# Feature maps scaled crosswise, sets normalised in pairs, and a Gram certificate placed later, in a kernel that mixes linear and softmax attention

## The chip, the cores and the metric

The kernel runs on one core of a Trainium2 chip. The metric is the device time of one execution in microseconds (us). The engines are PE (matrix multiplication; PEld is its weight loading), DVE (the vector engine), ACT (activations), POOL (GpSimd) and SP, which issues transfers.

## What is computed

Two attention layers read the same x (2048 tokens, 512 features, 32 heads of 16) and a gate mixes them for each token.

```python
def reference(A_x, A_wqkv, A_w_phi, A_wo, B_x, B_wqkv, B_wo, gate_w):
    x = A_x
    g = _sigmoid((x * gate_w).sum(-1, keepdims=True))
    # A, linear attention; q, k, v = heads of x @ A_wqkv
    pq, pk = q @ w_phi, k @ w_phi                      # per head
    phi_q = concat([softmax(pq), softmax(-pq)], -1)    # 16 + 16 features
    phi_k = concat([softmax(pk), softmax(-pk)], -1)
    kv, z = phi_k^T v, phi_k.sum(keys)
    a = (phi_q kv) / (phi_q z + 1e-6) @ A_wo
    # B, softmax attention; q, k, v = heads of x @ B_wqkv
    b = softmax(q k^T / 4) v @ B_wo
    return g * a + (1 - g) * b
```

## The kernel before

**Softmax attention in sets.** The work is cut into 32 sets. A set is one chunk of 512 queries, one group of eight heads and, of these, the four of one parity. A set has 16 blocks, one for each 128 keys. For a block PE computes the scores of four heads (L1241) into PSUM; then the exponential is taken in one of two ways. On ACT it is two activations of 128x1024 (L1256), followed by one round of four value matmuls (L1292). On DVE it is four tensor_scalar ops of 128x512 (L1261) that write the bits of an approximate exponential as int16 into a tile T; two copies of T with a constant added to the bits follow, the "shifts", each either on DVE (L1273, 128x2048 int16) or on POOL (L1276, 128x1024 int32); and three rounds of value matmuls, two of them with scaled values vS made on POOL (L968), average the three approximations. For up to six blocks of a set, and for each shift, both variants are written down, and the planner keeps one. At the end of a set the sums in psO are evicted (L876), transposed by a transfer (L1204, OT to OTT), divided by the row sum in column 16 of each head by a reciprocal (L1182) and a product (L1184), and after two sets transposed again for the output projection (L1320).

**Linear attention beside it.** `phi` (L1077) makes the feature map of 128 tokens: a projection with the merged weight Wp = A_wqkv w_phi (L893), two exponentials on ACT (L1084, of p and of -p), a tree of four adds on POOL (L1090, L1095, L1096, L1097) that gives the 64 sums of a row (32 heads, two halves), a reciprocal on DVE (L1099) and a product on POOL (L1100). It runs 16 times for keys (w = 1) and 16 times for queries (w = 0). For a query tile the map is transposed by a transfer (L1154), multiplied with kz, which holds kv and z (L1160), and divided: an add of 1e-6 with the gate's exponential ez (L1164), a reciprocal (L1167), two products (L1168). The gate g is ez = exp(-logit) (L1002), and three small DVE ops make 1 - g (omg, L1003 to L1005).

**The certificate.** Exponentials are taken without subtracting a maximum, so the kernel bounds the scores from the norms of rows of x, columns of W_Bq and W_Bk, columns of Wp and the gate's weight. `sumsq` (L1023) squares 128x1024 pieces on POOL (L1028, 16 of them), sums them over partitions with 32 matmuls against ones (L1033), and reduces on DVE (L1041, L1046, L1051). Ten small DVE ops (L1065 to L1075) make a flag; at the end each engine branches to a general path (`_general`) if the bounds do not hold.

**What sets the order.** Nothing is ordered by hand. `_Sched` plans the five engines ahead of time: each operation has an engine, a due time `prio`, a cost `occ` in us and dependencies, and the planner places them one by one by earliest start and due time. Due times are written in sets,

```python
P_SET = 20.9
T0 = 10.5
    def st_(x):
        return T0 + P_SET * x
```

and the constants GT, WP0, CX0, CW0, CP0, PK0, PK1, PQ0 to PQ3, OF0 place gate, merged weights, certificate, key maps, query maps and output projections in these units. `SHP` is the planned cost of a shift on POOL, `SWITCH` that of changing PE's tiling between scores, value rounds and full matmuls. A DVE operation of kind "sh" (shifts and normalising products) and a POOL operation are never planned at once, and each POOL operation gets a dependency on the last such DVE operation before it. `STYLES` holds one seed for each window of 3 us; a seed other than 0 draws the planner's tolerances at random for that window. The emitted program is the planned order on each engine, with semaphore waits for the dependencies, so each engine works strictly in that order.

Of the kernel before, what the change touches and what calls it, by code (L numbers as in the profile page):

```python
# [723 lines left out]
def _build(ctx, nc, A_x, A_wqkv, A_w_phi, A_wo, B_wqkv, B_wo, gate_w, out):  # L724
# [280 lines left out]
    op_omg = add("dve", st_(GT), 0.15, lambda e: e.tensor_tensor(omg[:], omg[:], ez[:], ALU.mult), deps=[op_g2], kind="sh")  # L1005

# [16 lines left out]
    def sumsq(prio, src, deps, name):  # L1023
        m = _Tile(M_r)
        sq = []
        for hh in range(2):
# [1 line left out]
            sq.append((b, pool(prio, 2.0, lambda e, b=b, hh=hh: e.tensor_tensor(  # L1028
                b.ap.rearrange("p (t c) -> p t c", t=2), src(hh), src(hh), ALU.mult), list(deps) + op_qz[0, 0], name="sq" + name, tiles=[b], nb=prio - 6.0)))

        f = None
        for hh in range(2):
            calls = [lambda e, t=t: e.matmul(m.ap, lhsT=ones[:], rhs=sq[t // 2][0].ap[:, 512 * (t % 2):512 * (t % 2) + 512],  # L1033
                                             start=(t == 0), stop=(t == KT - 1)) for t in (2 * hh, 2 * hh + 1)]
# [4 lines left out]
    for c in range(QC):
        m, f = sumsq(st_(CX0 + 0.3 * c), lambda hh, c=c: xT[:, 2 * hh:2 * hh + 2, NQ * c:NQ * (c + 1)], op_x[c], "x")  # L1040
        cert.append(add("dve", st_(CX0 + 0.2 + 0.3 * c), 0.62, lambda e, m=m, c=c: e.tensor_reduce(ct[:, c:c + 1], m.ap, AX.X, ALU.max),  # L1041
                        deps=[f], tiles=[m]))
    for i, (w, dp) in enumerate(((W_Bq, [op_wq[0], op_wq[1]]), (W_Bk, [op_wk[0], op_wk[1]]))):
        m, f = sumsq(st_(CW0 + 0.3 * i), lambda hh, w=w: w[:, 2 * hh:2 * hh + 2, :], dp, "w")
        use_wk.append(f)
        cert.append(add("dve", st_(CW0 + 0.2 + 0.3 * i), 0.62, lambda e, m=m, i=i: e.tensor_reduce(  # L1046
            ct[:, 16 + 32 * i:48 + 32 * i], m.ap.rearrange("p (h d) -> p h d", d=16), AX.X, ALU.add), deps=[f], tiles=[m]))
    for w in range(2):
        m, f = sumsq(st_(CP0 + 0.3 * w), lambda hh, w=w: Wp[:, w, 2 * hh:2 * hh + 2, :], ev_wp[w], "p")
        (use_wp0, use_wp1)[w].append(f)  # L1050
        cert.append(add("dve", st_(CP0 + 0.2 + 0.3 * w), 0.62, lambda e, m=m, w=w: e.tensor_reduce(  # L1051
            ct[:, 4 + w:5 + w], m.ap, AX.X, ALU.max), deps=[f], tiles=[m]))
# [418 lines left out]
```

## Time and profile before

| what | us |
|---|---|
| median of 3 runs | 702.51 (701.68 to 703.22) |
| the profiled execution | 703.81 |
| its span, first to last instruction | 702.0 |

The profile is of one execution, so durations read from it add up to its own time; 1.8 us lie outside the span. A row of a group gives the line, the engine, the operation, output and input tiles with their shapes, the count, then busy time and the mean of one instruction in ns, and then the engine's idle time just before these and who ended it. Busy time counts an overlap of two instructions of an engine once, so busy time divided by the count can be less than the mean. A row of waits reads: engine, tile and line that waited, whom it waited for, us in total, times, longest.

### The profile page before, as it was taken

Reading aid. Unit: us, or ns where it says so; the run is one execution under the profiler, and the core shown is the slowest. Engines: PE = TensorE matmul, PEld = TensorE weight load, DVE = VectorE, ACT = ScalarE, POOL = GpSimd, SP = SyncE. Lnnn points to the kernel's source line nnn. Section 1 sums busy time; section 2 is a strip of 40 time slices with the busy share of each in tenths; the row PEclk is TensorE's granted clock in tenths of the full one; section 3 lists DMA queues with packets and bytes.
Section 4 is the critical chain, followed back from the end, with each engine's and each line's share of the span. In section 5 each row is a group of like instructions: output and inputs, shape, how many; then the busy total and the mean of one; then the engine's idle time right before and its main releaser. Section 6 shows DMA issues by size and latency. Waiting matters only on the chain.

```text
span 702.0 us, 16145 instructions
## 1 busy us (share of the span) xinstructions
PE 656.6 (94%) x6616; PEld 208.9 (30%) x6616; DVE 672.3 (96%) x1208; ACT 672.4 (96%) x759; POOL 454.2 (65%) x377
## 2 busy tenths in 40 slices
PE   8999999999999999988999999989999999998996
PEld 3333443342323222222222232222222222222222
DVE  5899999999999999999999999999999999999995
ACT  6989989999999999999999999999999999999994
POOL 6365776654766546566677556668675676778773
PEclk8999999999999999999999999999999999999999
DMA  6500000011000000011122212113121221110001
GB/s 159 143 17 9 8 17 16 17 41 37 17 16 16 10 13 13 10 23 23 36 46 35 46 35 49 39 39 47 31 45 27 44 53 24 39 39 16 17 8 35
DMA packets 72192, 23.80 MB, mean 34 GB/s; under 512 B 64048, under 2 KB 72112, under 8 KB 72112
## 3 DMA queue, kind: packets, MB, share of 16 engines
q1 hardware_dynamic: 70896, 21.93, 15.0%
q8 instruction: 53, 0.87, 0.5%
q10 hardware_dynamic: 1216, 0.79, 0.4%
q14 instruction: 27, 0.22, 0.1%
HBM read 4.21 MB, written 2.10 MB: 9 GB/s over the span
## 4 chain that ended last, share of the span: by engine, by line
ACT 66%; PE 20%; DVE 11%; DMA 1%; issue 1%; POOL 0%; DVEq 0%
ACT E L1256 62%; PE psR L1241 7%; DVE T L1261 6%; PE psO L1292 6%; PE psR L893 3%; DVE TS L1273 2%; PE psR L1336 2%; ACT WAT L1084 2%; ACT phk L1084 2%; DMA OTT<-OT 1%; PE psR L955 1%; PE psR L907 1%; DVE vB L960 0%; DVE kT L876 0%; DVE ct L1041 0%
## 5 line engine op out<-in xcount | busy, mean ns | idle before, releaser
L1256 ACT ACTIVATE E<-psR 128x1024 bf16<-128x1024 f32 x682 | 640.5, 1104 | 14.5 <-PE psR L1241 12.0
L1261 DVE TENSOR_SCALAR T<-psR 128x512 int16<-128x512 f32 x684 | 432.8, 677 | 8.6 <-PE psR L1241 5.4
L1241 PE MATMUL psR<-qz,kT 32*128 32x512 bf16 (+1 forms) x2048 | 296.6, 386 | 36.0 <-ACT E L1256 28.1
L1276 POOL TENSOR_TENSOR TS<-T,shc 128x1024 int32<-128x1024 int32 x140 | 263.2, 1893 | 73.7 <-DVE TS L1273 47.1
L1241 PEld LDWEIGHTS psR<-qz,kT 32*128 32x128 bf16 (+1 forms) x2048 | 78.1, 91 | 288.7 <-ACT E L1256 218.5
L1273 DVE TENSOR_SCALAR TS<-T 128x2048 int16<-128x2048 int16 x202 | 132.7, 687 | 1.0 <-PE psO L1292 0.8
L1292 PE MATMUL psO<-E,vB 128*18 128x512 bf16 x1364 | 125.9, 381 | 0.3
L1292 PE MATMUL psO<-TS,vS 128*18 128x512 bf16 x1368 | 119.8, 383 | 0.2
L1292 PE MATMUL psO<-T,vB 128*18 128x512 bf16 x684 | 67.0, 382 | 0.0
L1100 POOL TENSOR_TENSOR WAT<-WAT,ss 128x1024 bf16<-128x1024 bf16 x16 | 30.9, 1931 | 32.4 <-DVE TS L1273 32.4
L1095 POOL TENSOR_TENSOR tr<-WAT 128x256 f32<-128x256 f32 x32 | 23.3, 729 | 40.8 <-DVE TS L1273 39.3
L1100 POOL TENSOR_TENSOR phk<-phk,ss 128x1024 bf16<-128x1024 bf16 x16 | 30.9, 1930 | 27.9 <-DVE TS L1273 27.8
L1292 PEld LDWEIGHTS psO<-E,vB 128*18 128x18 bf16 x1364 | 31.3, 88 | 48.8 <-issue 36.9
L1292 PEld LDWEIGHTS psO<-TS,vS 128*18 128x18 bf16 x1368 | 29.0, 87 | 51.2 <-issue 32.7
L893 PE MATMUL psR<-xT,WB 128*128 128x512 bf16 x128 | 34.0, 389 | 0.3 <-DVE T L1261 0.2
L893 PE MATMUL psR<-Wp,xT 128*128 128x512 bf16 x128 | 33.1, 381 | 0.5 <-DMA Wp<-WAT 0.3
L968 POOL TENSOR_SCALAR vS<-vB 128x144 bf16<-128x144 bf16 (+1 forms) x32 | 12.7, 399 | 20.4 <-DVE TS L1273 16.4
L1090 POOL TENSOR_TENSOR WAT<-phk 128x512 f32<-128x512 bf16 x16 | 18.4, 1156 | 11.5 <-DVE TS L1273 8.1
L1090 POOL TENSOR_TENSOR WAT<-WAT 128x512 f32<-128x512 bf16 x16 | 18.5, 1156 | 8.6 <-DVE TS L1273 6.5
L1292 PEld LDWEIGHTS psO<-T,vB 128*18 128x18 bf16 x684 | 16.6, 87 | 19.0 <-issue 15.6
L876 DVE CAST OT<-psO 128x512 bf16<-128x512 f32 x31 | 21.0, 678 | 0.0
L1028 POOL TENSOR_TENSOR phk<-xT 128x1024 bf16<-128x1024 bf16 x8 | 15.2, 1894 | 9.0 <-DVE TS L1273 7.2
(114 smaller groups left out, 402.7 us busy)
## 6 DMA issues: line engine op xcount, KB each, us to landing
qz<-qst SPq DMA_DIRECT2D x120, 16.0 KB, 1.8
out_dram<-WAv SPq DMA_DIRECT2D x12, 128.0 KB, 1.7
WB<-in_B_wqkv_dram SPq DMA_DIRECT2D x3, 384.0 KB, 5.5
T<-in_A_x_dram SPq DMA_DIRECT2D x2, 256.0 KB, 4.3
T<-in_A_x_dram ACTq DMA_DIRECT2D x2, 256.0 KB, 4.6
WAv<-in_A_wqkv_dram SPq DMA_DIRECT2D x1, 512.0 KB, 6.7
WB<-in_A_wo_dram SPq DMA_DIRECT2D x1, 512.0 KB, 3.5
WB<-in_B_wo_dram SPq DMA_DIRECT2D x1, 512.0 KB, 4.4
```

Of the source, the lines that this page charges most:

```text
L876: return add("dve", prio, 0.6, lambda e: e.tensor_copy(dst(), src()), deps=deps, tiles=tiles, name=name)
L893: calls = [lambda e, t=t: e.matmul(tile.ap[:, off:off + 512], lhsT=lhs(t), rhs=rhs(t), start=(t == 0), stop=(t == KT - 1)) for t in range(KT)]
L1084: ex = [add("act", prio, 0.48, lambda e, s=s: e.activation(ev()[:, :, 16 * s:16 * s + 16], P(), ACTF.Exp, scale=1.0 - 2.0 * s), deps=[f] + ...
L1090: p1 = pool(prio + 2, 1.23, lambda e: e.tensor_tensor(v8(), eg()[:, :, 0:8], eg()[:, :, 8:16], ALU.add), ex + use_wat, tiles=[ee, tr], nam ...
L1095: p2 = pool(prio + 2, 0.92, lambda e: e.tensor_tensor(u4(), v8()[:, :, 0:4], v8()[:, :, 4:8], ALU.add), [p1], tiles=[tr, tr2])
L1100: return pool(prio + 6, 1.95, lambda e: e.tensor_tensor(eg(), eg(), ss.ap[:, 1, :].unsqueeze(2).to_broadcast([128, 64, DH]), ALU.mult), [o ...
L1241: ins = e.matmul(rs[h].ap, lhsT=kT[a:a + n, g, 128 * kt:128 * (kt + 1)], rhs=qt.ap[a:a + n, c, :], start=True, stop=True, tile_position=(a ...
L1256: exps.append(add("act", pr + 0.5 * cc, 0.905, lambda e, rs=rs, E=E: e.activation(E.ap.rearrange("p (a n) -> p a n", n=512), pair(rs), ACT ...
L1261: exps.append(add("dve", pr + 0.5 * cc + 0.01 * h, 0.6, lambda e, rs=rs, T=T, cc=cc, h=h: e.tensor_scalar(T.ap[:, 1024 * cc + 512 * h:1024 ...
L1273: sh.append([add("dve", pr + 1.0 + 0.3 * m, 0.6, lambda e, T=T, X=X, m=m: e.tensor_single_scalar(X.ap, T.ap, SHIFT[m], ALU.add), deps=exps ...
L1276: sh[-1].append(pool(pr + 1.0 + 0.3 * m, SHP, lambda e, T=T, X=X, m=m: e.tensor_tensor(X.ap.bitcast(I32), T.ap.bitcast(I32), shc[:, m - 1: ...
L1292: ins = e.matmul(O.ap[32 * col:32 * col + VW, :], lhsT=lhs(hd), rhs=rhs(cc)[:, 512 * h:512 * (h + 1)], start=(first_pv[s] == key), stop=(l ...
```

## The change

- **Query maps.** For w = 0 the last add on POOL writes the sum of the p half to the place of the -p half and the other way round, in two ops; the reciprocal is gone and the map is multiplied by the other half's sum. Both halves so carry the factor (sum of p) x (sum of -p), which numerator and denominator share. The 1e-6 is put into kz, once, by a three-operand op with a column `eps` made by two small POOL ops.
- **Division of a query tile.** One reciprocal reads the denominators from PSUM, one three-operand product over 512 columns multiplies by ez and by it. ez is now exp(logit), and omg = 1 / (1 + ez), so the product with ez is gone. The general path takes gate and omg accordingly.
- **Normalisation.** Both sets of a pair are transposed into one tile, then one reciprocal (32 columns) and one product (512 columns) serve both; sets 30 and 31 stay by themselves. OTT and rB have one slot of double size instead of two.
- **Certificate.** For each piece PE makes four 128x128 Gram blocks, 16 matmuls of 128 columns each, 128 in all, in place of squares and sums; the largest entry is the largest squared norm. DVE reduces as before, four small transfers lay four columns of 128 numbers on one partition, and ten DVE ops make the flag from a coarser bound. It is due at sets 13 to 16 instead of 1.2 to 3.7.
- **Plan.** Planned costs of POOL ops and of the switch are lowered, due times of gate, key maps, query maps and the first output projection are moved, and STYLES is another list (231 entries, before 234).

```diff
-GT = 2.2
+GT = 3.2
 WP0 = 2.4
-CX0, CW0, CP0 = 1.2, 2.6, 3.4
-PK0, PK1 = 4.4, 0.5
-PQ0, PQ1, PQ2, PQ3 = 13.0, 0.75, 16.45, 0.95
-OF0 = 16.8
+CX0, CW0, CP0 = 15.2, 14.0, 13.0
+PK0, PK1 = 4.4, 0.6
+PQ0, PQ1, PQ2, PQ3 = 14.6, 0.7, 17.6, 0.9
+OF0 = 17.6
...
-SWITCH = 0.11
+SWITCH = 0.105
...
-Q32, PSH, SHP = 1, 1, 1.88
+Q32, PSH, SHP = 1, 1, 1.86
...
-            self.give = r.uniform(0.0, 5.0)
+            self.give = r.uniform(1.0, 8.0)
...
-    OTT_r = ring(2, [128, 4, 128], name="OTT")
-    rB_r = ring(2, [128, 4, 4], F32, name="rB")
+    OTT_r = ring(1, [128, 2, 4, 128], name="OTT")
+    rB_r = ring(1, [128, 2, 4, 4], F32, name="rB")
...
-                op_vS[g, c, m] = pool(prio + 1, 0.42 * len(ds) + 0.05, lambda e, m=m, a=a, b=b: e.tensor_scalar(
+                op_vS[g, c, m] = pool(prio + 1, 0.12 * len(ds) + 0.18, lambda e, m=m, a=a, b=b: e.tensor_scalar(
...
-    op_ge = add("act", st_(GT), 0.3, lambda e: e.activation(ez[:], tg.ap[:, 0:NT], ACTF.Exp, scale=-1.0), deps=gops, tiles=[tg])
+    op_ge = add("act", st_(GT), 0.3, lambda e: e.activation(ez[:], tg.ap[:, 0:NT], ACTF.Exp), deps=gops, tiles=[tg])
...
-    def sumsq(prio, src, deps, name):
+    def gram(prio, src, deps, name, col):
         m = _Tile(M_r)
...
+        calls = [lambda e, i=i, t=t: e.matmul(m.ap[:, 128 * i:128 * (i + 1)], lhsT=src(t, i), rhs=src(t, i), start=(t == 0), stop=(t == KT - 1))
+                 for i in range(4) for t in range(KT)]
+        f = chain(prio, calls, 0.056, deps, [m], "gr" + name, max(0.0, prio - EARLY), 2 * PIECE)
+        cert.append(add("dve", prio + 2, 0.62, lambda e: e.tensor_reduce(ct[:, col:col + 1], m.ap, AX.X, ALU.max), deps=[f], tiles=[m]))
+        return f
...
+    c3 = [add("sp", pc + 1, 0.63, lambda e, i=i, j=j: e.dma_start(mrow()[:, 128 * i:128 * (i + 1)], ct[:, j:j + 1]), deps=[c1, c2], tiles=[most], name="most",
+              dma=4.0, lane=lambda: ("most", 0)) for i, j in enumerate((8, 9, 6, 7))]
+    pc += 8
...
-        p1 = pool(prio + 2, 1.23, lambda e: e.tensor_tensor(v8(), eg()[:, :, 0:8], eg()[:, :, 8:16], ALU.add), ex + use_wat,
+        p1 = pool(prio + 2, 1.14, lambda e: e.tensor_tensor(v8(), eg()[:, :, 0:8], eg()[:, :, 8:16], ALU.add), ex + use_wat,
...
-        p2 = pool(prio + 2, 0.92, lambda e: e.tensor_tensor(u4(), v8()[:, :, 0:4], v8()[:, :, 4:8], ALU.add), [p1], tiles=[tr, tr2])
-        p3 = pool(prio + 2, 0.56, lambda e: e.tensor_tensor(u2(), u4()[:, :, 0:2], u4()[:, :, 2:4], ALU.add), [p2], tiles=[tr2])
-        p4 = pool(prio + 2, 0.48, lambda e: e.tensor_tensor(ss.ap[:, 0, :], u2()[:, :, 0], u2()[:, :, 1], ALU.add), [p3],
-                  tiles=[tr2, ss])
-        o7 = add("dve", prio + 5, 0.46, lambda e: e.reciprocal(ss.ap[:, 1, :], ss.ap[:, 0, :]), deps=[p4], tiles=[ss])
-        return pool(prio + 6, 1.95, lambda e: e.tensor_tensor(
+        p2 = pool(prio + 2, 0.72, lambda e: e.tensor_tensor(u4(), v8()[:, :, 0:4], v8()[:, :, 4:8], ALU.add), [p1], tiles=[tr, tr2])
+        p3 = pool(prio + 2, 0.4, lambda e: e.tensor_tensor(u2(), u4()[:, :, 0:2], u4()[:, :, 2:4], ALU.add), [p2], tiles=[tr2])
+        u1 = lambda i: u2()[:, :, i].rearrange("p (h s) -> p s h", s=2)
+        so = lambda: ss.ap[:, 0, :].rearrange("p (h s) -> p s h", s=2)
+        p4 = [pool(prio + 2, 0.28, lambda e: e.tensor_tensor(ss.ap[:, 0, :], u2()[:, :, 0], u2()[:, :, 1], ALU.add), [p3], tiles=[tr2, ss])
+              ] if w else [pool(prio + 2, 0.22, lambda e, s=s: e.tensor_tensor(so()[:, 1 - s], u1(0)[:, s], u1(1)[:, s], ALU.add), [p3],
+                                tiles=[tr2, ss]) for s in range(2)]
+        if w == 0:
+            return pool(prio + 6, 1.9, lambda e: e.tensor_tensor(
+                eg(), eg(), ss.ap[:, 0, :].unsqueeze(2).to_broadcast([128, 64, DH]), ALU.mult), p4, tiles=[ee, ss], name="phi")
+        o7 = add("dve", prio + 5, 0.46, lambda e: e.reciprocal(ss.ap[:, 1, :], ss.ap[:, 0, :]), deps=p4, tiles=[ss])
+        return pool(prio + 6, 1.9, lambda e: e.tensor_tensor(
...
-        o4 = add("dve", prio + 12, 0.16, lambda e, nv=nv, rA=rA, st=st: e.tensor_scalar(
-            rA.ap.rearrange("p (b g c) -> p b g c", b=2, g=4), nv()[:, :, :, 64:68], 1e-6, ez[:, st:st + 1], op0=ALU.add, op1=ALU.mult),
-            deps=[o3, op_ge], tiles=[rA] + nd, name="den")
-        o5 = add("dve", prio + 12, 0.26, lambda e, rA=rA: e.reciprocal(rA.ap, rA.ap), deps=[o4], tiles=[rA])
-        o8 = [add("dve", prio + 13, 0.34, lambda e, b=b, nd=nd, rA=rA, oA=oA: e.tensor_tensor(
...
+        o5 = add("dve", prio + 12, 0.28, lambda e, nv=nv, rA=rA: e.reciprocal(
+            rA.ap.rearrange("p (g c) -> p g c", c=4), nv()[:, :, 64:68]), deps=[o3], tiles=[rA] + nd, name="den")
+        o8 = [add("dve", prio + 13, 0.62, lambda e, nv=nv, rA=rA, oA=oA, st=st: e.scalar_tensor_tensor(
+            oA.ap.rearrange("p (g h d) -> p g h d", h=4, d=DH), nv()[:, :, 0:64].rearrange("p g (h d) -> p g h d", d=DH),
+            ez[:, st:st + 1], rA.ap.rearrange("p (g h) -> p g h", h=4).unsqueeze(3).to_broadcast([128, 8, 4, DH]),
+            op0=ALU.mult, op1=ALU.mult), deps=[o5, op_ge] + use_wav, tiles=nd + [rA, oA], name="oA")]
...
+            elif par == 0:
+                norm.append(n2)
+            else:
+                n2 = [norm.pop(), n2]
+                both = lambda: tt.ap.rearrange("p a i (s c) -> p a (i s) c", c=32)
+                n3 = add("dve", pr + 2, 0.28, lambda e: e.reciprocal(rb.ap.rearrange("p a b c -> p a (b c)"), both()[:, :, :, 16]), deps=n2,
+                         tiles=[tt, rb])
+                norm.append(add("dve", pr + 2, 0.6, lambda e: e.tensor_tensor(
+                    ob.ap.rearrange("p i (s a d) -> p a (i s) d", a=2, d=16), both()[:, :, :, 0:16],
+                    rb.ap.rearrange("p a b c -> p a (b c)").unsqueeze(3).to_broadcast([128, 2, 16, 16]), ALU.mult),
+                    deps=[n3], tiles=[tt, rb, ob], name="norm", kind="sh"))
```

More of the change, by code (lines that the diff above doesn't have):

```diff
@@ L23 @@
 SCALE = 0.25
-LIMIT2 = 50.0 ** 2
+LIMIT2, LIMIT2P = 50.0 ** 2, 10.0 ** 2
 VW = 18
@@ L552, in _general @@
     gate, omg = ns.mtmp[:, 0, 0:NT], ns.mtmp[:, 1, 0:NT]
-    g1 = add("dve", lambda e: e.tensor_scalar(gate, ns.ez[:], 1e30, 1.0, op0=ALU.min, op1=ALU.add))
-    g2 = add("dve", lambda e: e.reciprocal(gate, gate), [g1])
-    g3 = add("dve", lambda e: e.tensor_scalar(omg, gate, -1.0, 1.0, op0=ALU.mult, op1=ALU.add), [g2])
+    g1 = add("dve", lambda e: e.tensor_scalar(omg, ns.ez[:], 1e30, 1.0, op0=ALU.min, op1=ALU.add))
+    g2 = add("dve", lambda e: e.reciprocal(omg, omg), [g1])
+    g3 = add("dve", lambda e: e.tensor_scalar(gate, omg, -1.0, 1.0, op0=ALU.mult, op1=ALU.add), [g2])
     wat = add("sp", lambda e: e.dma_start_transpose(WAT[:], ns.A_wqkv[:, 0:2 * D]), dma=True)
@@ L1038, in _build @@
     cert = []
     for c in range(QC):
[L1040 to L1047, printed above, removed]
+        gram(st_(CX0 + 0.3 * c), lambda t, i, c=c: xT[:, t, NQ * c + 128 * i:NQ * c + 128 * (i + 1)], op_x[c], "x", c)
@@ L1048, in _build @@
+    for k, (w, dp) in enumerate(((W_Bq, [op_wq[0], op_wq[1]]), (W_Bk, [op_wk[0], op_wk[1]]))):
+        use_wk.append(gram(st_(CW0 + 0.3 * k), lambda t, i, w=w: w[:, t, 128 * i:128 * (i + 1)], dp, "w", 6 + k))
     for w in range(2):
[L1049 to L1052, printed above, removed]
+        (use_wp0, use_wp1)[w].append(gram(st_(CP0 + 0.3 * w), lambda t, i, w=w: Wp[:, w, t, 128 * i:128 * (i + 1)], ev_wp[w], "p", 4 + w))
@@ L1072, in _build @@
[L1072 to L1075 removed]
+    c2 = add("dve", pc, 0.15, lambda e: e.tensor_reduce(ct[:, 9:10], ct[:, 4:6], AX.X, ALU.max), deps=cert)
@@ new lines, in _build @@
+    c3 = [add("sp", pc + 1, 0.63, lambda e, i=i, j=j: e.dma_start(mrow()[:, 128 * i:128 * (i + 1)], ct[:, j:j + 1]), deps=[c1, c2], tiles=[most], name="most",
+              dma=4.0, lane=lambda: ("most", 0)) for i, j in enumerate((8, 9, 6, 7))]
+    pc += 8
+    c4 = add("dve", pc, 0.4, lambda e: e.tensor_reduce(ct[0:1, 10:14], mrow().rearrange("p (a b) -> p a b", a=4), AX.X, ALU.max), deps=c3, tiles=[most])
+    c5 = add("dve", pc, 0.15, lambda e: e.tensor_tensor(ct[0:1, 11:12], ct[0:1, 11:12], ct[0:1, 16:17], ALU.max), deps=[c4], kind="sh")
@@ L1077, in phi @@
+    c9 = add("dve", pc, 0.15, lambda e: e.tensor_single_scalar(ct[0:1, 14:16], ct[0:1, 11:13], LIMIT2, ALU.is_le), deps=[c8])
+    c9 = add("dve", pc, 0.15, lambda e: e.tensor_scalar(ct[0:1, 8:9], ct[0:1, 14:15], ct[0:1, 15:16], None, op0=ALU.mult), deps=[c9])
+    op_flag = add("dve", pc, 0.15, lambda e: e.tensor_scalar(flag[0:1], ct[0:1, 8:9], -1.0, 1.0, op0=ALU.mult, op1=ALU.add), deps=[c9])
     def phi(prio, w, st, ee, ee_deps):
@@ L1181, in normal @@
         def normal(eng_deps, sl, tv, occ, tt=tt):
-            n3 = add("dve", pr + 2, 0.17, lambda e: e.reciprocal(rb.ap[:, sl], tv()[:, sl, :, 16]), deps=eng_deps, tiles=[tt, rb])
+            n3 = add("dve", pr + 2, 0.17, lambda e: e.reciprocal(rb.ap[:, par, sl], tv()[:, sl, :, 16]), deps=eng_deps, tiles=[tt, rb])
             n = sl.stop - sl.start
@@ L1302, in _build @@
         end = s == N_SETS - 1
-        ot, tt, rb = _Tile(OT_r), _Tile(M_r if end else OTT_r), _Tile(rB_r)
+        if par == 0:
+            both, rb = _Tile(OTT_r), _Tile(rB_r)
+        ot, tt = _Tile(OT_r), _Tile(M_r) if end else both
         halves = finish(s, par, pr, end, O, ot, tt, rb, ob, pvs, norm)
```

69 lines of the change are left out of this document (27 added, 42 removed), and 28 rows, old and new, of the table STYLES.

## The prediction

> **What bounds the kernel now.** I read the page's engine line first, then busy time by stretches, then the groups of instructions, then the waits.
>
> ```profile
> PE 656.6 (94%) x6616; PEld 208.9 (30%) x6616; DVE 672.3 (96%) x1208; ACT 672.4 (96%) x759; POOL 454.2 (65%) x377
> ```
>
> VectorE (DVE) and ScalarE (ACT) are level at 96%, so neither alone is the bound: a gain on one counts only as far as work can be passed between them. The stretches (columns: window, length, then busy us of PE, PEld, DVE, ACT and POOL with instruction counts, clock, DMA) show where that fails:
>
> ```profile
> 20.00:100.00 80.00, 77.92 (x866) 30.93 (x862) 76.86 (x133) 72.35 (x78) 49.94 (x41) 0.98 0.14 36
> 100.00:270.00 170.00, 163.66 (x1645) 53.24 (x1637) 168.33 (x303) 168.23 (x196) 102.42 (x100) 1.00 0.08 20
> 270.00:360.00 90.00, 82.13 (x848) 23.51 (x846) 88.58 (x161) 90.00 (x105) 58.35 (x47) 1.00 0.13 25
> 600.00:650.00 50.00, 45.40 (x485) 13.15 (x482) 49.55 (x91) 49.92 (x56) 38.39 (x25) 1.00 0.13 27
> 650.00:690.00 40.00, 38.03 (x399) 10.68 (x398) 38.11 (x65) 39.89 (x45) 30.05 (x17) 1.00 0.05 11
> ACT E L1256 <- PE psR L1241: 7.2, 14, 1.3
> PEld psR L1241 <- ACT E L1256: 218.5, 506, 0.8
> ```
>
> From 100 us on ACT idles under 2 us in 170, and nothing in 270 to 360. Only 20 to 100 us is different: ACT idles 80 − 72.35 = 7.65 us, and the first wait row, taken from that window, gives 7.2 us of it to PE's scores. PE is 97% busy there, so there PE ends the wait. Over the whole span PE waits for ACT instead (last row, 218.5 us). So the time is ACT and DVE together, plus PE in one early stretch.
>
> **The exchange rate.** A block (128 keys, 4 heads, 512 queries) goes either to ACT or to DVE, and the planner chooses for up to six of a set's 16.
>
> ```profile
> L1256 ACT ACTIVATE E<-psR 128x1024 bf16<-128x1024 f32 x682 | 640.5, 1104 | 14.5 <-PE psR L1241 12.0 <-PE psO L1292 1.0
> L1261 DVE TENSOR_SCALAR T<-psR 128x512 int16<-128x512 f32 x684 | 432.8, 677 | 8.6 <-PE psR L1241 5.4 <-POOL TS L1276 0.3 <-PE psO L1292 0.3
> L1273 DVE TENSOR_SCALAR TS<-T 128x2048 int16<-128x2048 int16 x202 | 132.7, 687 | 1.0 <-PE psO L1292 0.8
> L1276 POOL TENSOR_TENSOR TS<-T,shc 128x1024 int32<-128x1024 int32 x140 | 263.2, 1893 | 73.7 <-DVE TS L1273 47.1 <-PE psO L1292 10.3 <-DVE ob L1184 10.1
> L1292 PE MATMUL psO<-TS,vS 128*18 128x512 bf16 x1368 | 119.8, 383 | 0.2
> ```
>
> On ACT it is two activations, 2 × 640.5/682 = 1.88 us. On DVE it is four of 432.8/684 = 0.633, plus two shifted copies, of which 202 of 342 run on DVE at 132.7/202 = 0.657: 2.53 + 2 × 0.59 × 0.657 = 3.31 us. If ACT gains a and DVE gains d, then x = (d − a)/(1.88 + 3.31) blocks pass from ACT to DVE and the time falls by a + 1.88x. Each passed block costs PE two more rounds of four value matmuls, 8 × 119.8/1368 = 0.70 us.
>
> **Part by part: DVE (d).**
>
> ```profile
> L1099 DVE RECIPROCAL ss<-ss 128x64 f32<-128x64 f32 x32 | 17.3, 541 | 0.0
> L1164 DVE TENSOR_SCALAR rA<-psR,ez 128x32 f32<-128x32 f32 x16 | 3.8, 237 | 0.2 <-PE psR L1160 0.2
> L1167 DVE RECIPROCAL rA<-rA 128x32 f32<-128x32 f32 x16 | 5.5, 346 | 0.2
> L1168 DVE TENSOR_TENSOR WAv<-psR,rA 128x256 bf16<-128x256 f32 x32 | 11.9, 413 | 0.1
> L1352 DVE SCALAR_TENSOR_TENSOR Wp<-psR,omg,Wp 128x512 bf16<-128x512 f32 x2 | 1.4, 748 | 0.6 <-PE psR L1348 0.6
> L1182 DVE RECIPROCAL rB<-OTT 128x16 f32<-128x16 bf16 x31 | 7.5, 241 | 2.0 <-DMA OTT<-OT 2.0
> L1184 DVE TENSOR_TENSOR ob<-OTT,rB 128x256 bf16<-128x256 bf16 x31 | 12.9, 416 | 0.0
> L1137 DVE TENSOR_TENSOR kz<-kvs,mask 128x512 bf16<-128x512 f32 x1 | 0.7, 683 | 0.0
> L1005 DVE TENSOR_TENSOR omg<-omg,ez 128x16 f32<-128x16 f32 x1 | 0.6, 631 | 0.0
> ```
>
> Query maps: the 16 reciprocals of the query half go, 16 × 0.541 = 8.7 us. Denominators: the add and gate (3.8), the reciprocal (5.5) and two products (11.9) are 21.2 us; in their place stand 16 reciprocals and 16 three-operand products. No row shows a reciprocal read from PSUM with gaps: bounds 0.241 and 0.541, I take the row of its size, 0.346. For the product 0.683 and 0.748 are the ends; I take 0.72, between them. 16 × 1.066 = 17.1, saving 4.1 (0.6 to 6.4 at the ends). Normalisation: 15 pairs of sets had 2 × (241 + 416) = 1.31 us each and get one reciprocal of 32 columns (0.346) and one product of 512; that lies between one and two of the 0.416 ops, and I take 0.683 from the 512-column product: 1.03, saving 15 × 0.28 = 4.2 (2.1 to 8.3). The gate loses the 0.6 us product. The small certificate chain keeps ten ops, one of them over 512 values; an estimate from the 512-column rows makes that 0.5 more. Direct sum: 8.7 + 4.1 + 4.2 + 0.1 = 17.1, ends 11.4 and 24.
>
> **POOL.**
>
> ```profile
> L1028 POOL TENSOR_TENSOR phk<-xT 128x1024 bf16<-128x1024 bf16 x8 | 15.2, 1894 | 9.0 <-DVE TS L1273 7.2 <-DVE ob L1184 1.6 <-PE psR L1033 0.2
> L1028 POOL TENSOR_TENSOR phk<-Wp 128x1024 bf16<-128x1024 bf16 x4 | 7.6, 1894 | 1.1 <-DVE TS L1273 1.0
> L1028 POOL TENSOR_TENSOR phk<-WB 128x1024 bf16<-128x1024 bf16 x4 | 7.5, 1894 | 1.2 <-DVE TS L1273 1.2
> L1097 POOL TENSOR_TENSOR ss<-tr 128x64 f32<-128x64 f32 x32 | 9.4, 293 | 7.0 <-DVE TS L1273 5.5
> ```
>
> The 16 squares go, 30.3 us. The last add of each query map becomes two crossed halves: between 0 and 0.293 more each, I take 0.17, 16 × 0.17 = 2.7. Two tiny ops for the epsilon add 0.4. So 27.2 us come free, nearly all in the early stretch (due at sets 1.2 to 3.7, 36 to 88 us by the planner's formula). They are worth DVE time only if POOL then takes shifts from DVE: none, or 27.2/1.88 = 14 of them, 9.2 us. POOL idles 80 − 49.94 = 30 us in that stretch as it is, so its time is not what is short: I take a quarter, 2.3. d = 17.1 + 2.3 = 19.4.
>
> **PE (a).**
>
> ```profile
> L1033 PE MATMUL psR<-phk,ones 128*128 128x512 bf16 x24 | 7.3, 384 | 0.0
> L1033 PE MATMUL psR<-phk,ones 128*128 128x512 bf16 x32 | 9.7, 384 | 0.0
> L955 PE MATMUL psR<-WB,xT 128*128 128x128 bf16 x256 | 18.0, 226 | 0.4 <-DVE T L1261 0.2
> ```
>
> The 32 sums of squares (9.7 us, of which the first row places 7.3 in 20 to 100) give way to 128 Gram matmuls with 128 columns; L955 has their form: 128 × 18.0/256 = 9.0 us. They land about sets 13 to 16, 282 to 350 us by the planner's formula, where PE idles 7.9 of 90 us and four query tiles move out to later sets. In the early stretch the freed 7.3 us let PE feed ACT; the gain lies between 0 and all 7.65, since the gate's matmuls and the projections stay near. I take half, a = 3.8. Cost in the later stretch: nothing, covered by those 7.9 us; without that cover up to 1.1 us (9.0 − 7.9).
>
> **Moved and added waits.** The four certificate transfers (one column each, issued by SP) wait for two DVE maxima. Behind them in SP's queue stand the query copies and transposes, which are issued about a set ahead, 20 us; cost nothing, at most one set's late copy, some 2 us.
>
> ```profile
> gw<-in_gate_w_dram SPq DMA_DIRECT2D x4, 0.2 KB, 4.6
> SPq L1204 <- DVE T L1261: 160.9, 19, 22.8
> OTT<-OT SPq DMA_TRANSPOSE x31, 2.3
> ```
>
> The nearest transfer takes 4.6 us to land, and SP's queue stands waiting for most of the span (the largest row alone is 160.9 us). The flag is due at set 18.2 and 8 us, near 400 us, some 300 before the end. With one slot for both transposed sets, a pair's first transpose must wait for the previous pair's product; that was issued a set earlier, against 2.3 us for a transpose. What is late next after the query reciprocals go: the multiplication on POOL follows its own adds directly, so no engine waits anew.
>
> **Sum.** x = (19.4 − 3.8)/5.19 = 3.0 blocks; gain 3.8 + 1.88 × 3.0 = 9.5 us. PE pays 3.0 × 0.70 + 9.0 − 9.7 = 1.4 us, hidden in its idle 45. The profiled execution took 703.8 (span 702.0, 1.8 around it), 1.3 above the median, so 694.3 on its own scale and 693.0 for the median of 702.5. With the low ends (a = 0, d = 11.4) the gain is 4.1; with the high ones short of DVE's (a = 7.65, d = 26.3) it is 14.4.
>
> **Rivals.** One: the split stays as it is, or the freed DVE time falls where nothing can be passed on. ACT, idle in no later stage, then gives only its early a: 3.8 us, 698.7. For it: the split is fixed when the order is written. Against: every one of up to six blocks per set may go either way, and ACT and DVE end level now.
>
> Two: POOL takes many more shifts.
>
> ```profile
> POOL TS L1276 <- DVE TS L1273: 47.1, 35, 2.6
> POOL tr L1095 <- DVE TS L1273: 39.3, 23, 2.5
> POOL WAT L1100 <- DVE TS L1273: 32.4, 12, 3.9
> PEld psO L1292 <- POOL TS L1276: 5.2, 20, 0.5
> ```
>
> POOL's longest waits are for shifts on DVE, with which the planner never lets it overlap. If that exclusion is what is short, its total now is 454.2 + 132.7 + 12.9 = 599.8 us, and a moved shift uses only 1.88 − 0.66 = 1.22 more of it, so 27.2 us could pay for 22 shifts, 14.5 us of DVE. Then d = 31.6, x = 5.4, and the gain is 3.8 + 10.1 = 13.9: 688.6. [...]
>
> Three, slower: POOL's planned times lose their padding (0.92 becomes 0.72 against 729 ns measured; the shift 1.86 against 1893), so its results come later than planned, and PE, in order, stops at the value matmuls of a late shift. The last row prices it: 20 stops, 0.26 us each. PE's own total would be 658.0 busy, 8.0 idle at head and tail (0 to 20 and 690 on), and 0.26 per stop: it passes 702.0 at about 138 stops, and with all 147 shifts it gives 704.2, 704.9 for the median. Against: at 600 to 650 us POOL is 77% busy and ACT still idles 0.08 us.
>
> ```profile
> L1095 POOL TENSOR_TENSOR tr<-WAT 128x256 f32<-128x256 f32 x32 | 23.3, 729 | 40.8 <-DVE TS L1273 39.3 <-DVE ob L1184 1.4
> 0.00:20.00 20.00, 17.89 (x114) 8.36 (x114) 10.48 (x22) 12.38 (x16) 13.93 (x34) 0.83 0.71 166
> 690.00:702.00 12.00, 6.07 (x42) 2.00 (x41) 5.04 (x10) 2.57 (x5) 1.57 (x1) 0.97 0.16 51
> ```
>
> That the change does not do what it says would be a certificate that fails and starts the general path; with rows of squared length near 512 × 0.0025 = 1.3 its bounds lie far below the limits, and I give it nothing.
>
> **Chances.** Forecast 0.55; rival one 0.18; two 0.14; no change 0.04; slower 0.09. A run tells 0.2% (1.4 us) from no change. Faster 0.87, same 0.04, slower 0.09. The range takes in rivals one and two with the bounds, 687.5 to 699.5, and leaves out the last two cases.
>
> **What would show it.** Right: ACT's idle in 20 to 100 us near 4; no 541 ns reciprocal under the query maps; L1256's count down by about 6, L1261's up by 12; PE near 95%; ACT and DVE still level. Wrong: DVE under 95% with ACT's count unchanged (rival one), POOL shifts over 155 (two), PE's waits for POOL shifts far over 5 us (three), or the new product well over 0.75 us.

## The result, and the profile after

| | before | after | ratio (95% interval) |
|---|---|---|---|
| median, 8 runs each | 703.31 us | 697.53 us | 0.9924 (0.9901 to 0.9947) |
| the same kernels beside other experiments (15 and 5 runs) | 704.61 us | 697.91 us | 0.9902 (0.9886 to 0.9919) |
| profiled execution: span | 702.0 us | 695.1 us | |

The kernel is 5 to 7 us faster by the ratios (a ratio is taken over the runs and is not that of the two medians); the forecast was 9.5. First the engine line of the page, then the stretches to hold against those of before (window, length, busy us of PE, PEld, DVE, ACT and POOL with counts, clock, DMA share, GB/s):

```profile
PE 656.6 (94%) x6760; PEld 213.9 (31%) x6760; DVE 656.6 (94%) x1111; ACT 661.1 (95%) x747; POOL 525.5 (76%) x433
```
```profile
0.00:20.00 20.00, 16.86 (x126) 8.16 (x126) 11.36 (x23) 14.04 (x18) 14.45 (x38) 1.00 0.75 178
20.00:100.00 80.00, 78.22 (x886) 31.18 (x887) 73.96 (x123) 71.82 (x79) 63.38 (x48) 0.96 0.15 33
270.00:360.00 90.00, 86.52 (x962) 29.98 (x962) 88.43 (x152) 90.00 (x104) 64.07 (x52) 1.00 0.12 26
100.00:650.00 550.00, 524.14 (x5401) 163.78 (x5401) 536.66 (x908) 543.97 (x619) 419.77 (x335) 1.00 0.15 30
650.00:695.10 45.10, 37.37 (x353) 10.80 (x349) 34.62 (x60) 31.30 (x36) 27.90 (x15) 0.93 0.08 20
```

Two more rows of the same view of the kernel before:

```profile
100.00:650.00 550.00, 516.71 (x5213) 156.98 (x5205) 541.83 (x981) 545.16 (x620) 358.68 (x288) 1.00 0.15 30
650.00:702.00 52.00, 44.09 (x436) 12.68 (x435) 43.15 (x75) 42.46 (x48) 31.62 (x17) 0.99 0.08 20
```

The span can be split on ACT, since busy and idle must add up to it. ACT's busy time fell from 672.4 to 661.1, by 11.3 us. Its idle time (length minus busy) went from 7.6 to 6.0 in the first 20 us, from 7.65 to 8.18 in 20 to 100, from 4.8 to 6.0 in 100 to 650, and from 9.5 to 13.8 at the end: 4.4 more. 11.3 − 4.4 = 6.9, the whole difference of the spans. So ACT's work shrank by more than was forecast, and 4.3 us were lost again after 650 us. The 1.6 us won in the first 20 us are not the change's: the clock there was 0.83 in the one execution and 1.00 in the other, and a second profile of the kernel after has 0.83 and an idle of 7.7 too, while the kernel before without its query reciprocals (an experiment below) has 1.00 and 5.4. Without them the spans differ by 5.3 us. The groups say where the work went:

```profile
L1264 ACT ACTIVATE E<-psR 128x1024 bf16<-128x1024 f32 x670 | 629.5, 1105 | 14.5 <-PE psR L1249 8.0
L1269 DVE TENSOR_SCALAR T<-psR 128x512 int16<-128x512 f32 x708 | 447.3, 680 | 14.4 <-PE psR L1249 9.6
L1284 POOL TENSOR_TENSOR TS<-T,shc 128x1024 int32<-128x1024 int32 x194 | 364.3, 1891 | 55.9 <-DVE TS L1281 39.7
L1281 DVE TENSOR_SCALAR TS<-T 128x2048 int16<-128x2048 int16 x160 | 107.6, 705 | 0.5
```
```profile
L1098 DVE RECIPROCAL ss<-ss 128x64 f32<-128x64 f32 x16 | 8.7, 542 | 0.0
L1163 DVE RECIPROCAL rA<-psR 128x32 f32<-128x32 f32 x16 | 5.5, 345 | 0.3 <-PE psR L1159 0.2
L1165 DVE SCALAR_TENSOR_TENSOR WAv<-psR,ez,rA 128x512 bf16<-128x512 f32 x16 | 11.9, 744 | 0.3
L1209 DVE RECIPROCAL rB<-OTT 128x32 f32<-128x32 bf16 x15 | 5.0, 335 | 1.3 <-DMA OTT<-OT 1.3
L1211 DVE TENSOR_TENSOR ob<-OTT,rB 128x512 bf16<-128x512 bf16 x15 | 10.9, 725 | 0.0
```

Activations fell by 12, that is six blocks passed to DVE, not three. POOL makes 194 shifts, not 140 (about 147 was forecast), and DVE 160, not 202, though six more blocks need twelve more. Yet DVE idles 695.1 − 656.6 = 38.5 us, against 29.7 before: it is no longer level with ACT.

### The profile page after: what moved, and what is told of

It reads as the page before. It is cut to its first block, busy times and chain, and to the rows that moved or that the text cites. A ratio compares the mean times of both kernels' runs of the same rounds, so it can differ in the third digit from the quotient of the medians.

```text
span 695.1 us, 16428 instructions
## 1 busy us (share of the span) xinstructions
PE 656.6 (94%) x6760; PEld 213.9 (31%) x6760; DVE 656.6 (94%) x1111; ACT 661.1 (95%) x747; POOL 525.5 (76%) x433
## 4 chain that ended last, share of the span: by engine, by line
ACT 63%; PE 26%; DVE 6%; POOL 2%; DMA 2%; issue 1%; POOLq 0%; DVEq 0%
ACT E L1264 59%; PE psR L1249 9%; PE psO L1300 8%; PE psR L896 4%; DVE T L1269 3%; PE psR L1346 2%; ACT WAT L1077 2%; POOL TS L1284 2%; DMA OTT<-OT 2%; PE psR L958 2%; ACT phk L1077 2%; DVE TS L1281 1%; PE psR L910 1%; DVE ob L1211 0%; DVE OT L879 0%
## 5 line engine op out<-in xcount | busy, mean ns | idle before, releaser
L1264 ACT ACTIVATE E<-psR 128x1024 bf16<-128x1024 f32 x670 | 629.5, 1105 | 14.5 <-PE psR L1249 8.0
L1269 DVE TENSOR_SCALAR T<-psR 128x512 int16<-128x512 f32 x708 | 447.3, 680 | 14.4 <-PE psR L1249 9.6
L1284 POOL TENSOR_TENSOR TS<-T,shc 128x1024 int32<-128x1024 int32 x194 | 364.3, 1891 | 55.9 <-DVE TS L1281 39.7
L1249 PE MATMUL psR<-qz,kT 32*128 32x512 bf16 (+1 forms) x2048 | 292.2, 386 | 28.1 <-ACT E L1264 21.1
L1300 PE MATMUL psO<-TS,vS 128*18 128x512 bf16 x1416 | 125.3, 382 | 2.1 <-POOL TS L1284 1.4
L1300 PE MATMUL psO<-E,vB 128*18 128x512 bf16 x1340 | 122.2, 381 | 0.0
L1281 DVE TENSOR_SCALAR TS<-T 128x2048 int16<-128x2048 int16 x160 | 107.6, 705 | 0.5
L1300 PE MATMUL psO<-T,vB 128*18 128x512 bf16 x708 | 69.2, 381 | 0.0
L1077 ACT ACTIVATE WAT<-psR 128x512 bf16<-128x512 f32 x32 | 18.9, 697 | 0.0
L1089 POOL TENSOR_TENSOR tr<-tr 128x128 f32<-128x128 f32 x32 | 12.7, 398 | 7.8 <-DVE TS L1281 7.0
```

The costliest lines, as they stand in the source:

```text
L1077: ex = [add("act", prio, 0.48, lambda e, s=s: e.activation(ev()[:, :, 16 * s:16 * s + 16], P(), ACTF.Exp, scale=1.0 - 2.0 * s), deps=[f] + ...
L1249: ins = e.matmul(rs[h].ap, lhsT=kT[a:a + n, g, 128 * kt:128 * (kt + 1)], rhs=qt.ap[a:a + n, c, :], start=True, stop=True, tile_position=(a ...
L1264: exps.append(add("act", pr + 0.5 * cc, 0.905, lambda e, rs=rs, E=E: e.activation(E.ap.rearrange("p (a n) -> p a n", n=512), pair(rs), ACT ...
L1269: exps.append(add("dve", pr + 0.5 * cc + 0.01 * h, 0.6, lambda e, rs=rs, T=T, cc=cc, h=h: e.tensor_scalar(T.ap[:, 1024 * cc + 512 * h:1024 ...
L1281: sh.append([add("dve", pr + 1.0 + 0.3 * m, 0.6, lambda e, T=T, X=X, m=m: e.tensor_single_scalar(X.ap, T.ap, SHIFT[m], ALU.add), deps=exps ...
L1284: sh[-1].append(pool(pr + 1.0 + 0.3 * m, SHP, lambda e, T=T, X=X, m=m: e.tensor_tensor(X.ap.bitcast(I32), T.ap.bitcast(I32), shc[:, m - 1: ...
```

## The experiments

The theory: after the change ACT alone is the bound. Part of the gain was lost in two spots, behind the gate's matmuls at 90 to 100 us, where PE's clock falls to 0.66, and in the tail. The rival: ACT and DVE are still level, and the missing gain is lateness spread over the span, with PE stopping for late POOL shifts. Every edit but the tail's leaves the planned order as it was. That is also the limit of the study: undoing one part in the planner draws the whole order anew, with seeds chosen for another one, so no part of the change was undone in that way, and what the new seeds alone are worth was not measured.

**The gate, wider** (kernel after; the activation that reads the gate then takes every 32nd column, which is not shown).

```diff
-                    ins = e.matmul(tg.ap[:, st:st + 1], lhsT=xT[:, t, 128 * st:128 * (st + 1)], rhs=gw[:, t:t + 1],
+                    n = 64 if st < NT - 1 else 32
+                    ins = e.matmul(tg.ap[:, 32 * st:32 * st + n], lhsT=xT[:, t, 128 * st:128 * (st + 1)], rhs=gw[:, t:t + 1].to_broadcast([128, n]),
```

> The kernel after, with each gate matmul 64 columns wide instead of 1 (the gate's column repeated; only one column is read), the planned order unchanged. In the profile after, the granted clock falls to 0.66 at 90 to 100 us, right behind the gate's matmuls, and ACT idles 4.6 of those 10 us. [...] Rival (the missing gain is lateness spread over the span, PE waiting for POOL's shifts; the dip is made good later): under 1 us, ratio 0.992.

Measured: 0.9887 (0.9871 to 0.9903), 1.1 to 2.6 us faster than the kernel after, by its two ratios: less than the 3 to 4 us (0.987) that the theory put on the clock behind the gate, more than the rival's under 1 us (0.992). The intervals overlap with those of the kernel after, so this run alone does not settle that there is a gain; the same edit on the kernel before, further down, does. In the timeline of ACT (start, length, what, and in brackets the idle time before it) the kernel after reads

```profile
95.01 1.02 ACT L1264 ACTIVATE E<-psR 128x1024 bf16<-128x1024 f32 x1 [0.81 <-PE psR L1249]
99.83 2.85 ACT L1264 ACTIVATE E<-psR 128x1024 bf16<-128x1024 f32 x3 [3.80 <-PE psO L1300]
```

and with the wide gate

```profile
94.31 1.02 ACT L1265 ACTIVATE E<-psR 128x1024 bf16<-128x1024 f32 x1 [0.41 <-PE psR L1250]
97.77 2.86 ACT L1265 ACTIVATE E<-psR 128x1024 bf16<-128x1024 f32 x3 [2.44 <-PE psO L1301]
```

The stretches of 2 us show the clock (the column after POOL), first of the kernel after, then with the wide gate:

```profile
92.00:94.00 2.00, 2.00 (x40) 1.25 (x39) 1.50 (x3) 2.00 (x3) 1.72 (x1) 0.50 0.00 0
96.00:98.00 2.00, 2.00 (x16) 1.15 (x13) 0.76 (x2) 0.03 (x1) 0.39 (x1) 0.50 0.00 0
```
```profile
92.00:94.00 2.00, 1.75 (x31) 0.98 (x27) 1.35 (x3) 1.90 (x3) 1.89 (x1) 1.00 0.00 0
96.00:98.00 2.00, 2.00 (x29) 0.65 (x28) 1.60 (x4) 0.23 (x1) 1.47 (x3) 1.00 0.00 0
```

So in these two executions the clock cost 0.81 + 3.80 − 0.41 − 2.44 = 1.8 us. The 2.4 us that stay are put down to the order: ACT's wait ends at value matmuls (psO), and PE's timeline with the wide gate has two projections in a row ahead of them and of the next scores.

```profile
94.20 1.07 PE L958 MATMUL psR<-WB,xT 128*128 128x128 bf16 x16
95.10 0.24 PE L1048 MATMUL psR<-gw,ones 128*128 128x1 bf16 x4
95.39 1.04 PE L896 MATMUL psR<-xT,WB 128*128 128x512 bf16 x4
```

**The last block on ACT** (kernel after).

```diff
-        todo = [...] + [("dve", (i + 0.1) / 5.3, kt) for i, kt in enumerate(dset)]
+        todo = [...] + [("dve", (i + 0.1) / 5.3, kt) for i, kt in enumerate(dset) if (s, kt) != (31, 13)]
-            alt = (((s, kt), eng),) if kt in dset else ()
+            alt = (((s, kt), eng),) if kt in dset and (s, kt) != (31, 13) else ()
```

> The kernel after, with block 13 of the last set held on ACT, as in the kernel before; the planned order is the same up to the last 17 us. In the profile after, ACT's last exponential ends 8.7 us before its next work, in the one before 4.2, because the last block is on DVE, with one shift on DVE and the other on POOL behind it. Theory (4.5 us of the forecast gain went into the tail): ACT's gap falls back to about 4.5, 3 to 4 us faster than the kernel after, ratio to before about 0.987. Rival (the tail is bound by the evictions and the last projection, whatever block is last): under 1 us, ratio 0.992.

Measured: 0.9856 (0.983 to 0.9882), 3.2 to 4.8 us faster than the kernel after, as the theory has it. ACT's end in the three kernels, before, after and with the block on ACT:

```profile
675.21 15.72 ACT L1256 ACTIVATE E<-psR 128x1024 bf16<-128x1024 f32 x17
695.14 0.37 ACT L1317 COPY oBT<-psR 128x256 bf16<-128x256 bf16 x1 [4.21 <-PE psR L1310]
```
```profile
665.68 13.99 ACT L1264 ACTIVATE E<-psR 128x1024 bf16<-128x1024 f32 x15
688.35 0.37 ACT L1327 COPY oBT<-psR 128x256 bf16<-128x256 bf16 x1 [8.69 <-PE psR L1320]
```
```profile
659.28 21.30 ACT L1264 ACTIVATE E<-psR 128x1024 bf16<-128x1024 f32 x23
683.72 0.37 ACT L1327 COPY oBT<-psR 128x256 bf16<-128x256 bf16 x1 [3.14 <-PE psR L1320]
```

In the kernel after ACT has nothing left from 679.7 us on, while the last block goes through four ops and a shift on DVE and then a shift on POOL, which ends at 685.7 (quoted in the last section).

**A little more work on each engine** (kernel after): one extra op in each of the 16 query tiles, with a result that nothing uses. The added calls, shortened:

```diff
+        # DVE, ahead of the product over 512 columns
+        e.reciprocal(scr[:, 0:64], ez, repeated to 64 columns)
+        # ACT, ahead of the first exponential of a query map
+        e.activation(scr[:], tile.ap, ACTF.Exp)
+        # POOL, ahead of the query map's product
+        e.tensor_tensor(scr[:, 0:184], ident32, ident32, ALU.add)
+        # PE, ahead of the matmuls with kz
+            for b in range(2):
+                e.matmul(nd[b].ap, lhsT=ptt.ap[:, 0, :], rhs=xT[:, 0, 0:512], start=True, stop=True)
```

> The kernel after with one more reciprocal of 64 columns on DVE in each of the 16 query tiles, into a tile that nothing reads: 16 x 0.54 = 8.7 us of DVE, about what the removed reciprocals took; the order is unchanged. Theory (ACT is the bound after the change, DVE has slack): 4 us slower than the kernel after at most, ratio to before up to 0.998. Rival (ACT and DVE still level, both full): 7 to 9 us slower, ratio 1.002 to 1.005.

> The kernel after with one more exponential of 512 columns on ACT in each of the 16 query tiles, into a tile that nothing reads: 16 x 0.59 = 9.4 us of ACT; the order is unchanged. Theory (ACT is the bound): 8 to 10 us slower than the kernel after, ratio to before 1.004 to 1.006. Rival (PE or POOL lateness sets the pace, ACT follows): under 5 us slower, ratio under 1.0.

> The kernel after with one more add of 184 fp32 columns on POOL in each of the 16 query tiles, into a tile that nothing reads, about 16 x 0.54 = 8.6 us of POOL; the order is unchanged. Theory (POOL, 76% busy, has room, and ACT sets the pace): under 2 us slower than the kernel after. Rival (the shifts' time, on POOL and on DVE never at once, is the short thing): 5 us slower or more.

> The kernel after with two more matmuls of 512 columns on PE in each of the 16 query tiles, written over by the ones that follow, 16 x 0.53 = 8.5 us of PE; the order is unchanged. Theory (PE mostly waits for ACT to free its banks): under 3 us slower than the kernel after. Rival (PE's 95% in the query stage is full): 7 to 9 us slower.

The ops as they ran, on DVE, ACT, POOL and PE, each from its own kernel:

```profile
L1166 DVE RECIPROCAL scr<-ez 128x64 f32<-128x64 f32 x16 | 8.7, 544 | 0.3
```
```profile
L1078 ACT ACTIVATE scr<-psR 128x512 f32<-128x512 f32 x16 | 11.1, 695 | 0.0
```
```profile
L1097 POOL TENSOR_TENSOR scr<-ident 128x184 f32<-128x184 f32 x16 | 7.9, 492 | 26.4 <-DVE TS L1284 24.0 <-DVE ob L1214 2.3
```
```profile
L1158 PE MATMUL psR<-xT,Wp 128*128 128x512 bf16 x32 | 9.6, 381 | 0.9 <-ACT E L1266 0.9
```

| extra work | ratio to before | against the kernel after |
|---|---|---|
| DVE 8.7 us | 0.9942 (0.9922 to 0.9963) | 1.3 to 2.8 us slower |
| ACT 11.1 us | 1.0013 (0.9992 to 1.0034) | 6.3 to 7.8 us slower |
| POOL 7.9 us | 0.9956 (0.9936 to 0.9976) | 3.8 us slower (its own group: 0.9902) |
| PE 9.6 us | 0.9903 (0.9886 to 0.992) | no change (the same group) |

ACT's microsecond costs 0.6 to 0.7, POOL's about 0.5, DVE's 0.15 to 0.3, PE's nothing, each from a difference that is uncertain by some 2 us. The theory holds for DVE and PE; on ACT the cost stays below the 8 to 10 us expected of it. It missed POOL: about half of the added time came through, where it expected under 2 us and the rival 5 or more. So by these figures ACT is the dearest engine after the change, but not the bound alone. In the stretch 270 to 650 us ACT's busy time falls from 376.2 (the kernel after) to 374.0:

```profile
270.00:650.00 380.00, 360.41 (x3733) 111.53 (x3729) 371.01 (x631) 376.20 (x427) 290.07 (x224) 1.00 0.19 36
```
```profile
270.00:650.00 380.00, 358.69 (x3704) 110.66 (x3704) 370.97 (x626) 373.99 (x423) 294.24 (x238) 1.00 0.18 36
```

PE's stops for a late POOL shift grew at the same time, over the whole span from 14.2 us (45 stops; the row is in the next section) to 17.2:

```profile
PEld psO L1303 <- POOL TS L1287: 17.2, 51, 1.0
```

So POOL's lateness seems to reach ACT by way of PE. Whether what makes POOL late is that shifts on POOL and on DVE are never planned at once, as the rival has it, is not shown.

**Parts of the change on the order of before.** Without the query reciprocals:

```diff
+    for o, p in gone:          # o: the reciprocal of a query map, p: its last add
+        sch.order["dve"].remove(o)
+        sch.ops.remove(o)
...
-            eg(), eg(), ss.ap[:, 1, :].unsqueeze(2).to_broadcast([128, 64, DH]), ALU.mult),
+            eg(), eg(), ss.ap[:, w, :].unsqueeze(2).to_broadcast([128, 64, DH]), ALU.mult),
```

> The kernel before in its own order, without the 16 reciprocals of the query maps (the maps are multiplied by the sums instead, so they are left unnormalised): 8.7 us less on DVE, the split of blocks unchanged. Theory (with the order fixed, ACT is the bound, and freed DVE time counts only when blocks pass over): 0 to 2 us faster, ratio to before 0.997 to 1.000. Rival (ACT and DVE bound each other at every step, so a shorter DVE counts by itself): 4 to 8 us faster, 0.989 to 0.994.

Measured: 1.0000 (0.9982 to 1.0018). 8.7 us of DVE work less are worth nothing by themselves, within 1.3 us.

With the certificate shrunk to 8 columns (DVE then reduces these 8 columns, repeated, which is not shown), with the gate widened as above, and with both:

```diff
-                b.ap.rearrange("p (t c) -> p t c", t=2), src(hh), src(hh), ALU.mult)
+                b.ap.rearrange("p (t c) -> p t c", t=2)[:, :, 0:8], src(hh)[:, :, 0:8], src(hh)[:, :, 0:8], ALU.mult)
...
-            calls = [lambda e, t=t: e.matmul(m.ap, lhsT=ones[:], rhs=sq[t // 2][0].ap[:, 512 * (t % 2):512 * (t % 2) + 512],
+            calls = [lambda e, t=t: e.matmul(m.ap[:, 0:8], lhsT=ones[:], rhs=sq[t // 2][0].ap[:, 512 * (t % 2):512 * (t % 2) + 8],
```

> The kernel before in its own order, with the certificate worked out over 8 columns of each piece instead of 512 (the rest of its squares, sums and matmuls is left out): about 28 us less on POOL and 9 us less on PE, nearly all in the first 110 us. The forecast's term: PE is the bound in that stretch, ACT's 7.65 us of idle halves, 3.8 us faster, ratio 0.9946. Rival (ACT's waits there come from the order and the gate's clock dip): under 1 us, 0.999 or more.

> The kernel before with each gate matmul 64 columns wide, its order unchanged. The clock of 0.83 at 70 to 80 us goes to 1.00. Theory: ACT idles 1.3 us less there, ratio 0.998. Rival (a dip costs nothing): 1.000.

> The kernel before with both edits: the certificate over 8 columns (the rest of its work left out) and the wide gate. It takes the clock out of the question of what the certificate's early work cost, since without the dense certificate matmuls the clock dipped lower (0.70 against 0.83 at 70 to 80 us). Theory (in a fixed order the certificate's work cost nothing): as the wide gate alone, 0.997 of before. Rival (its cost was there and the deeper dip ate it): 3 us faster than that, 0.993 or less.

Measured: 0.9999 (0.9986 to 1.0012) for the small certificate, 0.9971 (0.9959 to 0.9984) for the wide gate, 0.9964 (0.9947 to 0.9981) for both. The gate's clock dip cost 2 us even before the change: over 70 to 80 us the clock is 0.83 in the profile before and 1.00 with the wide gate. The certificate's early work cost nothing that these runs can tell: at most 1 us by the first interval, and 0.5 us, uncertain by 1.5, where the wide gate keeps the clock at 1.00 over 20 to 100 us. That the certificate's matmuls hold the clock up is not shown: over 70 to 80 us it is 0.70 with the small certificate, but 0.66 in the run without the query reciprocals, which has those matmuls. The waits of ACT for scores from 20 to 110 us, in the kernel before, with the small certificate, with the wide gate and with both:

```profile
ACT E L1256 <- PE psR L1241: 8.1, 16, 1.3
```
```profile
ACT E L1256 <- PE psR L1241: 7.8, 16, 1.3
```
```profile
ACT E L1257 <- PE psR L1242: 7.4, 14, 2.2
```
```profile
ACT E L1257 <- PE psR L1242: 5.7, 14, 0.7
```

The small certificate by itself leaves the scores as late as ever. With both edits the waits are 1.7 us shorter than with the wide gate alone; much of that may be the one wait of 2.2 us in the third row.

**Both repairs together** (kernel after, wide gate, last block on ACT; both edits above), beside the kernel after once more.

> The kernel after, unchanged, beside the other runs of this group, so that they can be held against it. Every theory: ratio to before 0.9924, within 0.990 to 0.995.

> The wide gate and block 13 of the last set on ACT together. Theory (two separate places, 80 us and 680 us into the span): the gains add, 0.9887 + 0.9856 - 0.9924 = 0.982 of before. Rival (both fill the same slack, or the gain lies in a general lateness): no better than the tail alone, 0.985 to 0.986.

Measured: 0.9902 (0.9886 to 0.9919) for the kernel after, 0.9839 (0.9819 to 0.9858) with both, 691.96 against 704.61 us. This beats both kernels, the one after by 4.4 us by the ratios (6.0 by the medians). Whether the gains add is not settled: 0.982 and 0.9856 both lie within the interval.

## Why the prediction was right, and short

- **The exchange was the right mechanism.** With a fixed split, freed DVE time gave 1.0000; in the change ACT lost six blocks, 11.3 us. Rival one's time, 698.7, lies nearer to the measured 697.5 than the forecast's 693.0, but by luck: its 3.8 us for the early stretch did not come, and its split did change. What drew the six blocks over, the removed work or the newly drawn order, was not taken apart.
- **The step that failed is the term a.** It put half of ACT's early idle, 3.8 us, down to PE's certificate work. Removing that work in the old order gave nothing by itself, and 0.5 us, uncertain by 1.5, with the clock kept at 1.00; in the change the idle of 20 to 100 us went from 7.65 to 8.18. "PE is 97% busy there, so there PE ends the wait" read a share as a limit: PE took 9.6 us more in the query stage, at 95%, for nothing, and its busy time from 270 to 650 us, where all 16 query tiles lie, rose by 2.6 us only (360.41 to 362.99). Some 2 us of the early idle are the clock behind the gate; in the one place looked at, 94 to 98 us, the rest was the order on PE. What delays the other early scores stays open.
- **The term d was too small, and with it x.** The direct prices held: 17.4 us for the divisions (17.1 forecast), (5.0 + 10.9)/15 = 1.06 for a normalised pair (1.03). But POOL took 54 more shifts where seven were allowed for, past the 155 named for rival two. So x was 6.0 blocks, not 3.0, and ACT's work fell by 11.3, not 5.7. This is rival two's sign and nearly its 5.4 blocks; its gain of 13.9 did not come, since it counted on a as well and on a tail that stays. Whether the removed squares or the lower planned costs made that room stays open.
- **The sum assumed that ACT and DVE end level.** They do not: DVE idles 8.8 us more than before.
- **The tail was left out.** The sum took the time after 650 us as fixed; it grew by 4.3 us because the last block went to DVE. Put in these numbers, the gain is 11.3 less 4.3 at the end and less 1.7 more idle from 20 to 650 us, 5.3, to which the start of these two executions adds 1.6; the sum had 3.8 + 5.7. That it lands as near as it does is in part luck: a and the tail took away most of what the larger d brought.
- **The covers held.** The Gram matmuls took 10.0 us (9.0 forecast), and from 270 to 360 us, where 112 of the 128 lie, ACT is busy 90.00 of 90. Rival three's stops grew from 20 to 45, far from the 138 that it needed (its 704.9 for the median should read 704.7, 704.2 + 1.8 − 1.3):

```profile
L1027 PE MATMUL psR<-xT 128*128 128x128 bf16 x64 | 5.0, 221 | 0.0
L1027 PE MATMUL psR<-Wp 128*128 128x128 bf16 x32 | 2.5, 221 | 0.0
L1027 PE MATMUL psR<-WB 128*128 128x128 bf16 x32 | 2.5, 221 | 0.0
PEld psO L1300 <- POOL TS L1284: 14.2, 45, 1.0
```

## What to carry to other kernels

Where work is dealt out between engines ahead of time, an op that is removed can pay nothing while the deal stays, as with the query reciprocals here: price it on the engine that ends the span, and split the span on that engine into busy and idle by stage. Test which engine binds by adding work to each in a fixed order before trusting its busy share. And look at the last block by itself: a rule that balances a whole span can leave the slow way to the end.
